# A routed two-layer MLP behind attention: logits of the last token tiles from x rows instead of a product of two weight matrices

## The chip, the cores and the metric

The kernel runs on one core of one Trainium2 chip. The metric is the device time of one execution in microseconds (us); lower is better.

## What is computed

Linear attention feeds a dense MLP (`w_in`, `w_out`), whose rows x feed a mixture of 8 experts. Each token goes to one expert: the token and expert with the largest logit are taken first, and an expert that has its 288 tokens is closed.

```python
def _moe_ref(x, w_in, w_out):
    h = x @ w_in
    g = h * np.clip(h + 3.0, 0.0, 6.0) / 6.0
    return g @ w_out
def _moe2_ref(x, w_gate, w1, w2):           # x: 2304 x 512, 8 experts, cap = 288
    logits = x @ w_gate
    order = np.argsort(-logits.flatten())
    for idx in order:                       # greedy: best pair first
        tok, e = idx // E, idx % E
        if assigned[tok] >= 0 or counts[e] >= cap: continue
        assigned[tok] = e; counts[e] += 1
    for e in range(E):
        mask = assigned == e
        out[mask] = np.maximum(x[mask] @ w1[e], 0.0) @ w2[e]
```

## The kernel before

All matrix products are split in three: each operand is a high and a low part, and `mm3` (lines 207 to 210) issues high by high, low by high, high by low. The program has four stages.

**Attention** (to about 200 us) leaves x transposed in `xT`, in 4 blocks of 512 tokens and a short one of 256. The 2304 tokens are 18 tiles of 128; tiles 16 and 17 are the short block.

**The dense MLP** runs over `steps`: five blocks by 16 slices f of the hidden width. A step (`step`, line 648) splits the next slice of `w_in` (`st_wi`: iH by ScalarE, iL by GpSimd) and of `w_out` (`st_wo`: oH, oL), does A (`st_A`: 12 matmuls into a buffer called kv or s, then r, the product, gH and gL by ScalarE and VectorE) and, two steps behind, B (`st_B`: 3 matmuls for each token tile into pj). After its last slice each tile's sum is copied out of PSUM to `xs` (`st_x`, line 568), of which there are XS = 3 buffers, and stored to `xd` in DRAM. PSUM has four pj buffers, one for each tile of a long block: the next block's B cannot begin on a buffer before its copy is done.

**Logits.** For tiles 0 to 13, `st_dot` (line 578) has VectorE multiply x with the eight columns of the gate (`wgb`) and sum, 8 instructions for each tile; they read `xs`, for tiles 12 and 13 the PSUM buffer itself. Tiles 14 to 17 (LT = 14) use x·w_gate = g·(w_out·w_gate). In block 1 `st_wgT` and `st_wgp` (lines 584 to 598) make w_out·w_gate: in each of 16 steps 4 transposes of `w_out` (L588), a copy by ScalarE (L590), 4 small matmuls (L596, 8 rows in the trace), and two small splits (L597, L598). In block 3 and the short block `st_lg` (line 600) then adds 2 matmuls in each step (L611, L612). So the logits of the short block are known once its g are: A keeps all of them (`kept`), and B of the short block is taken out of the steps and becomes `rest` (line 682), 96 matmuls (L696).

**Routing and experts.** `finds` (line 796) looks for the members of one expert after another. `begin` makes keys from the logits; `closest` (line 758) takes six rounds, five or six bits each: VectorE compares (cmp, L755), TensorE counts with 18 small matmuls (L771), VectorE tests (ge, L773), TensorE spreads the result (L776), VectorE takes it in (L780, L783). Then slots (L857, L858), one-hot rows (OH, L889), 18 small matmuls (L893) and the list of rows idx (L898). `finds` stops at names ("cmp5", "ge", "mem", "OH", "first"), and the tables GAP0 and GAP say after how many pieces of other TensorE work it is taken up again. For expert 0 the other work is `rest`: TensorE's order is as written there, so L696 stands between the rounds. At "mem" the first two parts of the expert's w1 are requested on SP; after "first" `fetch_x` gathers the expert's rows from `xd` by three indirect DMAs on GpSimd (L917) and then requests the other weights, behind a small VectorE instruction that needs the gathered rows (L923). `prep` transposes the rows (L943), and `mlp` runs the expert; the searches for the next experts stand between its matmuls (`visit`, line 1045). N1 = 6 pieces of the second search stand ahead of `prep`.

Of the kernel before, what the change touches and what calls it, by code (L numbers as in the profile page):

```python
# [6 lines left out]
F32 = mybir.dt.float32  # L7
F32R = mybir.dt.float32r
# [12 lines left out]
def fused(tc, q, k, v, omega, w_in, w_out, w_gate, w1, w2, out):  # L21
# [25 lines left out]
    HPF, RP, N1, GAP = 400, 30, 6, dict(cmp0=12, cmp5=4, cmp6=5, ge=1, mem=6, OH=7)  # L47
# [6 lines left out]
    with ctx:  # L54
# [23 lines left out]

        wgp = cp.tile([P, 16, 2, 8], F32R, name="wgp")
# [469 lines left out]
        keep, on_pool, on_dve = {}, [], []  # L549

        def kept(f):

            if f % 8 == 0:
                keep["H"] = xp.tile([P, 2048], F32, tag="x", name="gHk")
            if f % 4 == 0:
                keep["L"] = (xp.tile([P, 4, 2 * P], F32, tag="x4", name="gLk", bufs=1).rearrange("p c n -> p (c n)") if f == 0 else
                             mb.tile([P, 512, 2], I32, tag="stg", name="gLk", bufs=CV[0]).rearrange("p n w -> p (n w)"))
            n = 2 * P
            return (keep["H"].bitcast(F32R)[:, (f % 8) * n:(f % 8 + 1) * n], keep["L"].bitcast(F32R)[:, (f % 4) * n:(f % 4 + 1) * n])
# [8 lines left out]
        def st_x(t, acc):  # L568
# [15 lines left out]
        def st_wgT(f):  # L584
# [8 lines left out]
        def st_wgp(f, wT):
            pg = ps("tp")
            for c in range(4):
                nc.tensor.matmul(pg[:, :8], wT[:, c * P:(c + 1) * P], wgn[:, c], start=c == 0, stop=c == 3, skip_group_check=True)  # L596
            nc.scalar.copy(wgp[:, f, 0], pg[:, :8])  # L597
            nc.vector.tensor_tensor(wgp[:, f, 1], pg[:, :8], wgp[:, f, 0].bitcast(F32), ALU.subtract)  # L598

        def st_lg(i):  # L600

            ib, f = steps[i]
            gH, gL = gs[i]
            if "lg" not in keep:
                keep["lg"] = ps("tp")
            nl = (NT - LT) * P

            o = keep["lg"][:16, 0:nl - 2 * P] if ib < NB else keep["lg"][:16, nl - 2 * P:nl]
            w = wgp[:, f].rearrange("p a e -> p (a e)")
            c = slice((LT - 4 * ib) * P if ib < NB else 0, len(blocks[ib]) * P)  # L610
            nc.tensor.matmul(o, w, gH[:, c], start=f == 0, stop=False, skip_group_check=True)  # L611
            nc.tensor.matmul(o, w, gL[:, c], start=False, stop=f == NF - 1, skip_group_check=True)  # L612
            if ib == NB and f == NF - 1:
                t8 = mp.tile([16, nl], F32, name="lgT", bufs=1)
                nc.vector.tensor_copy(t8, keep["lg"][:16, :nl])
                pt = ps("tp")
                for j in range(NT - LT):
                    nc.tensor.transpose(pt[:, 16 * j:16 * j + 16], t8[:, j * P:(j + 1) * P], ident[:16, :16])
                p4 = pt[:, 0:16 * (NT - LT)].rearrange("p (t a e) -> p t a e", t=NT - LT, a=2)

                nc.vector.tensor_copy(lg[:, LT:NT], p4[:, :, 0])
                nc.vector.tensor_scalar(lg[:, 0:LT], lg[:, 0:LT], 0.0, None, ALU.add)
# [488 lines left out]
```

## Time and profile before

| | us |
|---|---|
| median of 3 runs (lowest, highest) | 967.49 (965.32, 973.01) |
| the profiled execution | 971.14 |
| its span, first to last instruction | 969.4 |
| TensorE busy in the span | 901.8 (93%) |
| VectorE, ScalarE, GpSimd busy | 641.6, 496.2, 466.8 |

Busy shares are means over stages: the attention, the five MLP blocks (about 200 to 651 us), the wait for the first expert's rows, and the eight experts (670 us to the end) have limits of their own. A matmul's row shows its length in the pipeline, longer than the distance to the next; costs on TensorE are read from start to start.

### The profile page before, as it was taken

The page shows a single profiled execution, that of the slowest core. Times are in us where ns is not written, and L with a number is a line of the kernel's source. Part 1 is how long each engine was busy: PE and PEld are TensorE (multiplying, and loading weights), DVE is VectorE, ACT ScalarE, POOL GpSimd, SP SyncE. Part 2 cuts the span into 40 slices and gives each one's busy share as a digit, 9 for nine tenths or more (in the row PEclk, how much of TensorE's full clock was granted, in tenths as well). Part 3 has the DMA queues.
Part 4 walks back from the last instruction along what each step waited for, and adds up shares of the span by engine and source line. Part 5 has one row for each costly group of instructions (what it writes and reads, how often), then busy time and mean ns, then how long its engine had stood idle before and what let it go on. Part 6 is the DMA issues. An engine that isn't in the chain of part 4 may idle for free. (4 is left out here: it accounts for less than half of the span.)

```text
span 969.4 us, 16981 instructions
## 1 busy us (share of the span) xinstructions
PE 901.8 (93%) x6135; PEld 787.7 (81%) x6135; DVE 641.6 (66%) x1666; ACT 496.2 (51%) x1091; POOL 466.8 (48%) x435
## 2 busy tenths in 40 slices
PE   7999799989999999999999999985998999999996
PEld 6998698967778888878887888864997888889996
DVE  4779889868876653496259427765866857858442
ACT  5777788955545444534452447522343433434552
POOL 6669756327653433545444546302433444436542
PEclk9999899999999999999999999995999999989999
DMA  8855432012400000010000001006615426326600
GB/s 198 225 158 164 132 109 67 23 66 73 148 19 33 11 1 1 1 44 1 1 33 12 0 1 44 1 11 199 208 45 181 141 86 216 127 104 231 216 25 25
DMA packets 74852, 81.93 MB, mean 85 GB/s; under 512 B 27016, under 2 KB 59784, under 8 KB 74640
## 3 DMA queue, kind: packets, MB, share of 16 engines
q1 hardware_dynamic: 71536, 71.15, 23.1%
q0 software_dynamic: 3072, 9.44, 3.1%
q8 instruction: 48, 0.79, 0.3%
q10 hardware_dynamic: 160, 0.26, 0.1%
q14 instruction: 36, 0.29, 0.1%
HBM read 71.39 MB, written 9.45 MB: 83 GB/s over the span
## 5 line engine op out<-in xcount | busy, mean ns | idle before, releaser
L502 POOL TENSOR_TENSOR iL<-W,iH 128x512 fp32r<-128x512 f32 x80 | 112.9, 1412 | 96.5 <-ACT iH L501 86.8
L962 POOL TENSOR_TENSOR iL<-We,iH 128x512 fp32r<-128x512 f32 x63 | 84.3, 1339 | 135.1 <-ACT iH L959 129.1
L208 PE MATMUL kv<-xH,iH 128*128 128x512 f32 (+2 forms) x376 | 132.4, 352 | 1.8 <-ACT xH L520 1.8
L210 PE MATMUL kv<-xH,iL 128*128 128x512 f32 (+2 forms) x376 | 129.4, 344 | 2.6 <-POOL iL L502 2.6
L209 PE MATMUL kv<-xL,iH 128*128 128x512 f32 (+2 forms) x376 | 129.2, 344 | 0.9 <-DVE xL L521 0.9
L510 POOL TENSOR_TENSOR oL<-W,oH 128x512 fp32r<-128x512 f32 x48 | 66.2, 1380 | 95.8 <-ACT oH L509 95.6
L208 PE MATMUL pj<-oH,gH 128*128 128x512 f32 x256 | 103.1, 403 | 3.5 <-DVE xs L570 3.5
L210 PE MATMUL pj<-oH,gL 128*128 128x512 f32 x256 | 101.6, 397 | 0.0
L209 PE MATMUL pj<-oL,gH 128*128 128x512 f32 x256 | 101.4, 396 | 0.0
L501 ACT CAST iH<-W 128x512 fp32r<-128x512 f32 x80 | 49.7, 621 | 82.7 <-PE kv L209 48.8
L581 DVE SCALAR_TENSOR_TENSOR junk<-xs,wgb 128x512 f32<-128x512 f32 x96 | 89.4, 962 | 2.3 <-PE tp L596 2.2
L273 ACT ACTIVATE kp<-pj,bias 128x128 f32<-128x128 f32 x288 | 79.4, 412 | 17.9 <-DVE bias L265 14.4
L208 PE MATMUL pj<-hH,oH 128*128 128x288 f32 x256 | 84.3, 329 | 0.0
L210 PEld LDWEIGHTS kv<-xH,iL 128*128 128x128 f32 x376 | 72.0, 191 | 11.3 <-POOL iL L502 4.3
L208 PEld LDWEIGHTS kv<-xH,iH 128*128 128x128 f32 x376 | 71.9, 191 | 11.2 <-issue 3.5
L209 PE MATMUL pj<-hL,oH 128*128 128x288 f32 x256 | 77.3, 302 | 3.2 <-DVE hL L984 3.2
L959 ACT CAST iH<-We 128x512 fp32r<-128x512 f32 x64 | 39.5, 619 | 79.0 <-PE kv L209 30.6
L209 PEld LDWEIGHTS kv<-xL,iH 128*128 128x128 f32 x376 | 72.1, 192 | 8.5 <-DVE xL L521 1.2
L544 DVE SCALAR_TENSOR_TENSOR kv<-r,kv 128x512 f32<-128x512 f32 (+1 forms) x54 | 34.7, 643 | 65.9 <-ACT r L543 65.7
L210 PE MATMUL pj<-hH,oL 128*128 128x288 f32 x256 | 76.7, 299 | 0.0
L182 POOL TENSOR_TENSOR stg<-cg,stg 128x512 f32<-128x512 f32 x32 | 41.8, 1305 | 71.6 <-issue 30.4
L509 ACT CAST oH<-W 128x512 fp32r<-128x512 f32 x80 | 49.5, 620 | 41.8 <-PE pj L210 25.7
(400 smaller groups left out, 2393.3 us busy)
## 6 DMA issues: line engine op xcount, KB each, us to landing
We<-in_moe_w_dram SPq DMA_DIRECT2D x64, 512.0 KB, 7.4
stg<-in_moe_w_in_dram SPq DMA_DIRECT2D x16, 512.0 KB, 4.9
stg<-in_moe_w_out_dram SPq DMA_DIRECT2D x16, 512.0 KB, 3.6
ld<-in_k_dram SPq DMA_DIRECT2D x8, 512.0 KB, 4.9
vf<-in_v_dram SPq DMA_DIRECT2D x32, 128.0 KB, 3.4
ld<-in_q_dram SPq DMA_DIRECT2D x8, 512.0 KB, 4.8
xd<-xs SPq DMA_DIRECT2D x16, 256.0 KB, 2.4
wgb<-wgd SPq DMA_DIRECT2D x1, 2048.0 KB
```

What stands on the lines that cost most here:

```text
L182: nc.gpsimd.tensor_tensor(lf, g.bitcast(F32), lf, ALU.mult)
L208: nc.tensor.matmul(o, aH, bH, start=first, stop=False, skip_group_check=True)
L209: nc.tensor.matmul(o, aH, bL, start=False, stop=False, skip_group_check=True)
L210: nc.tensor.matmul(o, aL, bH, start=False, stop=last, skip_group_check=True)
L273: nc.scalar.activation(kp[:, i, j], pjs[s // 4][:, s % 4], AF.Exp, bias=bias[:, i, j:j + 1])
L501: nc.scalar.copy(iH, wi)
L502: on_pool.append(nc.gpsimd.tensor_tensor(iL, wi, iH.bitcast(F32), ALU.subtract).ins)
L509: nc.scalar.copy(oH, wo)
L510: (nc.gpsimd if (ib > 0 if ib < NB else f >= OD) else nc.vector).tensor_tensor(oL, wo, oH.bitcast(F32), ALU.subtract)
L581: nc.vector.scalar_tensor_tensor(junk, x, 1.0, wgb[:, e], ALU.mult, ALU.mult, accum_out=d)
L959: nc.scalar.copy(iH, wi)
L962: (nc.vector if first and f == 0 else nc.gpsimd).tensor_tensor(iL, wi, iH.bitcast(F32), ALU.subtract)
```

## The change

The product w_out·w_gate and all that makes or uses it is gone. The short block runs like the others: A and B in the same step, g in the usual buffers. The logits of tiles 12, 13, 16 and 17 are now made from x rows by TensorE: `st_lT` transposes the row tile (4 transposes), copies it, and `st_lg` multiplies with the gate (4 matmuls). Tiles 12 and 13 are done in two steps of the short block; 16 and 17 after its end, with one copy on ScalarE and one on VectorE. Tiles 14 and 15 now go by VectorE from PSUM, as 12 and 13 did. The first search stands after all this, with nothing between its pieces. `xs` has four buffers. The x rows of tile 16 are stored on SP ahead of expert 0's first weights. N1 is 4, and GAP changes: 3 or 4 pieces after a compare, 2 after "ge", and at most 3 anywhere until two experts are found. In the short block oL alternates between GpSimd and VectorE.

```diff
-    OD, WG, ND, NE, XS = 16, 18, 3, 3, 3
-    LB, LL, GB = 2, 3, 3
-    LT = 14
-    GAP0 = dict(begin=32, cmp5=6, cmp6=7, ge=2, mem=9, OH=12)
+    ND, NE, XS = 3, 2, 4
+    LB, GB = 2, 3
+    LT = (12, 13, 16, 17)
-    HPF, RP, N1, GAP = 400, 30, 6, dict(cmp0=12, cmp5=4, cmp6=5, ge=1, mem=6, OH=7)
+    HPF, RP, N1, GAP = 400, 30, 4, dict(cmp0=12, cmp5=3, cmp6=4, ge=2, mem=6, OH=7)
...
-            (nc.gpsimd if (ib > 0 if ib < NB else f >= OD) else nc.vector).tensor_tensor(oL, wo, oH.bitcast(F32), ALU.subtract)
+            (nc.gpsimd if (ib > 0 if ib < NB else f % 2 == 0) else nc.vector).tensor_tensor(oL, wo, oH.bitcast(F32), ALU.subtract)
...
-            if t < 16:
-
-                if t < LT:
-                    dots.extend((acc if t >= 12 else x, lg[:, t, e:e + 1], e) for e in range(8))
+            if t in LT:
+                xrow.append((t, x))
+            else:
+
+                dots.extend((acc if t >= 14 else x, lg[:, t, e:e + 1], e) for e in range(8))
...
+        def st_lT(x, copy):
 
             pt = ps("big")
             for c in range(4):
-                nc.tensor.transpose(pt[:, c * P:(c + 1) * P], w_rows(f)[:, c * P:(c + 1) * P], ident)
...
+                nc.tensor.transpose(pt[:, c * P:(c + 1) * P], x[:, c * P:(c + 1) * P], ident)
+            xT = mp.tile([P, DM], F32, tag="junk", name="xTt", bufs=2)
+            copy(xT, pt)
+            return xT
+
+        def st_lg(t, xT):
+
             pg = ps("tp")
             for c in range(4):
...
+                nc.tensor.matmul(pg[:, :8], xT[:, c * P:(c + 1) * P], wgn[:, c], start=c == 0, stop=c == 3, skip_group_check=True)
+            nc.vector.tensor_scalar(lg[:, t], pg[:, :8], 0.0, None, ALU.add)
...
-                if ib == 1:
-                    wT = st_wgT(f)
+                if xrow:
+                    t, x = xrow.pop(0)
+                    xT = st_lT(x, nc.scalar.copy)
...
-            if LB <= i < NB * NF + LB:
-                if i - LB >= (NB - 1) * NF and LT < 4 * NB:
-                    st_lg(i - LB)
+            if LB <= i:
                 st_B(i - LB)
...
+            elif i + 1 - LB == len(steps):
+                st_dot(len(dots))
+                nc.vector.tensor_scalar(lg[:, 0:12], lg[:, 0:12], 0.0, None, ALU.add)
+                nc.vector.tensor_scalar(lg[:, 14:16], lg[:, 14:16], 0.0, None, ALU.add)
+                xTs = [st_lT(x, copy) for (t, x), copy in zip(xrow, (nc.scalar.copy, nc.vector.tensor_copy))]
+                for (t, x), xT in zip(xrow, xTs):
+                    st_lg(t, xT)
...
-            for _ in more:
...
+        with tc.manual_schedule(engines={ET.PE}), tc.high_priority(offset=400):
+            while True:
+                z = next(route)
+                if z == "mem":
+                    fetch_w(0, rs[0], 0, Z0)
+                if z == "first":
+                    break
...
-                wait[0] = GAP.get(z, 0)
+
+                wait[0] = min(GAP.get(z, 0), 3) if found[0] < 2 else GAP.get(z, 0)
```

Three places show what moves. TensorE, the end of the first round of the first search, before (tp holds the counts, pj the short block's sums):

```order
L771 LDWEIGHTS cmp_6575
L771 MATMUL tp_6584<-oh_6573,cmp_6575 32x8
L696 MATMUL pj_6500<-oL_6532,gHk_6034 128x512
L696 MATMUL pj_6500<-oH_6531,gLk_6184 128x512
L696 MATMUL pj_6499<-oH_6541,gHk_6034 128x512
L776 LDWEIGHTS onesu_4509
L776 MATMUL tp_6606<-ge_6604,onesu_4509 128x8
```

The same place now (L714 is L771 of before, L719 is L776):

```order
L714 LDWEIGHTS cmp_6458
L714 MATMUL tp_6467<-oh_6456,cmp_6458 32x8
L719 LDWEIGHTS onesu_4284
L719 MATMUL tp_6488<-ge_6486,onesu_4284 128x8
L714 LDWEIGHTS cmp_6494
L714 MATMUL tp_6496<-oh_6456,cmp_6494 32x8
```

The short block's B no longer stands between the pieces of the search.

VectorE at the start of block 2, before (L570 is the copy of a tile to xs, L581 a dot, L544 and L546 belong to A):

```order
L544 SCALAR_TENSOR_TENSOR kv<-r,kv 128x512
L570 COPY xs<-pj 128x512
L581 SCALAR_TENSOR_TENSOR junk,lg<-xs,wgb 128x512
L546 TENSOR_TENSOR gL<-kv,gH 128x512
L581 SCALAR_TENSOR_TENSOR junk,lg<-xs,wgb 128x512 x5
L544 SCALAR_TENSOR_TENSOR s_4621<-r,s_4621 128x512
L581 SCALAR_TENSOR_TENSOR junk,lg<-xs,wgb 128x512 x2
L546 TENSOR_TENSOR gL<-s_4621,gH 128x512
L570 COPY xs<-pj 128x512
```

The same place now (L548 is the copy, L562 a dot, L532 and L534 belong to A):

```order
L532 SCALAR_TENSOR_TENSOR kv<-r,kv 128x512
L548 COPY xs<-pj 128x512
L562 SCALAR_TENSOR_TENSOR junk,lg<-xs,wgb 128x512
L534 TENSOR_TENSOR gL<-kv,gH 128x512
L548 COPY xs<-pj 128x512
L562 SCALAR_TENSOR_TENSOR junk,lg<-xs,wgb 128x512 x4
```

The second copy stands behind one dot instead of eight.

VectorE in the second search, at the small instruction that needs the gathered rows (L923), before:

```order
L783 SCALAR_TENSOR_TENSOR v__7061<-v__7032,dk,dg 128x36
L755 TENSOR_TENSOR cmp<-v__7061,ta 128x576
L773 TENSOR_SCALAR ge<-tp 32x8
L923 SCALAR_TENSOR_TENSOR e_6950<-xg,ei 1x1
L780 TENSOR_REDUCE dk<-tp 128x1
```

The same place now (L866 is L923, L698 the compare, L716 the test):

```order
L723 TENSOR_REDUCE dk<-tp 128x1
L726 SCALAR_TENSOR_TENSOR v__6812<-v__6774,dk,dg 128x36
L866 SCALAR_TENSOR_TENSOR e_6730<-xg,ei 1x1
L698 TENSOR_TENSOR cmp<-v__6812,ta 128x576
L716 TENSOR_SCALAR ge<-tp 32x8
```

It moved from the third round to the second, ahead of that round's compare.

## Rows read from the trace of the kernel before

**Rows 1.** The page: granted TensorE clock in tenths, 40 slices of 24.2 us.
```profile
PEclk9999899999999999999999999995999999989999
```

**Rows 2.** Blocks 1, 2, 3: us, PE, PEld, DVE, ACT, POOL busy, clock, DMA, GB/s.
```profile
303.00:411.00 108.00, 108.00 (x561) 90.99 (x561) 59.04 (x138) 50.82 (x100) 45.17 (x55) 1.00 0.03 11
411.00:503.00 92.00, 90.23 (x385) 73.07 (x384) 54.46 (x102) 40.93 (x71) 44.65 (x33) 0.98 0.03 12
503.00:594.60 91.60, 89.85 (x417) 72.33 (x416) 54.70 (x103) 40.47 (x72) 44.46 (x33) 1.00 0.03 12
```

**Rows 3.** Timeline of TensorE in one step of block 1: start, length, instruction.
```profile
342.66 0.60 PE L588 MATMUL kv<-ident,W 128*128 128x128 f32 x4
343.01 0.48 PE L208 MATMUL pj<-oH,gH 128*128 128x512 f32 x1
...
345.88 0.95 PE L596 MATMUL tp<-wgn,wT 128*128 128x8 f32 x8
346.69 0.48 PE L208 MATMUL s<-xH,iH 128*128 128x512 f32 x1
```

**Rows 4.** Timeline of TensorE in block 2; in brackets idle before, and releaser.
```profile
421.94 0.50 PE L208 MATMUL pj<-oH,gH 128*128 128x512 f32 x1 [1.77 <-DVE xs L570]
...
451.97 0.39 PE L210 MATMUL s<-xH,iL 128*128 128x512 f32 x1
```

**Rows 5.** Timeline of VectorE in block 2.
```profile
421.21 0.68 DVE L570 COPY xs<-pj 128x512 f32<-128x512 f32 x1
...
448.62 0.69 DVE L546 TENSOR_TENSOR gL<-kv,gH 128x512 fp32r<-128x512 f32 x1 [0.66 <-ACT gH L545]
```

**Rows 6.** Groups of VectorE, 411 to 450 us: busy us, mean ns | idle before.
```profile
L581 DVE SCALAR_TENSOR_TENSOR junk<-xs,wgb 128x512 f32<-128x512 f32 x32 | 29.6, 973 | 0.0
```

**Rows 7.** Timeline of TensorE from the short block to the first expert.
```profile
596.53 0.28 PE L208 MATMUL kv<-xH,iH 128*128 128x256 f32 x1
...
599.41 0.28 PE L611 MATMUL tp<-gHk,wgp 128*16 128x256 f32 x1
...
599.64 0.28 PE L208 MATMUL kv<-xH,iH 128*128 128x256 f32 x1
...
630.34 0.59 PE L771 MATMUL tp<-oh,cmp 128*32 128x8 bf16 x18 [1.02 <-issue]
...
633.68 0.61 PE L771 MATMUL tp<-oh,cmp 128*32 128x8 bf16 x18
...
650.79 0.39 PE L696 MATMUL pj<-oH,gLk 128*128 128x512 f32 x1
...
659.54 0.64 PE L771 MATMUL tp<-oh,cmp 128*32 128x8 bf16 x18 [4.40 <-DVE cmp L755]
...
664.07 0.65 PE L771 MATMUL tp<-oh,cmp 128*32 128x8 bf16 x18 [1.04 <-DVE v__7061 L783]
...
668.16 0.90 PE L943 MATMUL kv<-ident,xg 96*128 96x96 f32 x4 [1.96 <-DMA xg<-xd,idx]
...
670.05 0.61 PE L208 MATMUL kv<-xH,iH 128*128 128x288 f32 x1
```

**Rows 8.** Timeline of VectorE in the first search.
```profile
626.78 0.30 DVE L728 TENSOR_REDUCE mx__6558<-lg 128x18 f32<-128x144 f32 x1
...
627.66 0.69 DVE L510 TENSOR_TENSOR oL<-W,oH 128x512 fp32r<-128x512 f32 x1 [0.57 <-ACT oH L509]
...
655.37 0.16 DVE L898 SCALAR_TENSOR_TENSOR idx<-tp,lo 96x3 int32<-96x3 f32 x1
```

**Rows 9.** Timeline of GpSimd at the first gather.
```profile
660.66 1.11 POOL L917 DMA_INDIRECT xg<-xd,idx  x1 [30.66 <-PE tp L776]
```

**Rows 10.** Timeline of TensorE at the second search's end.
```profile
687.55 0.19 PE L857 MATMUL tp<-mem,ta 128*128 128x36 bf16 x1
...
691.52 1.08 PE L893 MATMUL tp<-mv,OH 128*96 128x6 bf16 x18 [0.48 <-DVE OH L889]
```

**Rows 11.** Waits of TensorE, 672 to 930 us: us in total, times, longest.
```profile
PE tp L776 <- DVE ge L773: 4.8, 7, 1.9
```

More of the change, by code (lines that the diff above doesn't have):

```diff
@@ L547, in st_A @@
             gs[i] = gH, gL
[L549 to L559, printed above, removed]
+        on_pool, on_dve = [], []
         def x_rows(t):
@@ L594, in st_wgp @@
+        def st_lg(t, xT):
             pg = ps("tp")
             for c in range(4):
[L596 to L622, printed above, removed]
-                nc.vector.scalar_tensor_tensor(lg[:, LT:NT], p4[:, :, 1], 0.0, lg[:, LT:NT], ALU.add, ALU.add)
@@ L656, in step @@
                     st_w(i + 1)
-                if i + 2 - LB < NB * NF and i + 2 - LB > 0:
+                if i + 2 - LB > 0:
                     j = i + 2 - LB
@@ L671, in step @@
                         st_xb(ib + 1, c)
-            if LB <= i < NB * NF + LB:
-                if i - LB >= (NB - 1) * NF and LT < 4 * NB:
-                    st_lg(i - LB)
+            if LB <= i:
                 st_B(i - LB)
-            if i < len(steps) and ib == 1:
-                st_wgp(f, wT)
-            if i >= NB * NF + LL:
-                st_lg(i - LL)
-            st_dot((ND if i <= NB * NF else NE) if i < len(steps) else len(dots))
-        def rest():
-            base = NB * NF
-            for f in range(2):
-                wos[base + f] = st_wo(f)
-            a = [ps("acc") for _ in range(2)]
-            for f in range(NF):
-                if f + 2 < NF:
-                    wos[base + f + 2] = st_wo(f + 2)
-                gH, gL = gs[base + f]
-                oH, oL = wos.pop(base + f)
-                for j in range(2):
-                    c = slice(j * P, (j + 1) * P)
-                    for z, (x, y) in enumerate(((gH, oH), (gH, oL), (gL, oH))):
-                        nc.tensor.matmul(a[j], x[:, c], y, start=f == 0 and z == 0, stop=f == NF - 1 and z == 2, skip_group_check=True)
-                        if f == NF - 1 and z == 2:
-                            st_x(16 + j, a[j])
-                        yield
-        more = rest()
+            if i < len(steps):
+                if t is not None:
+                    st_lg(t, xT)
+                st_dot(ND if i <= NB * NF else NE)
+            elif i + 1 - LB == len(steps):
[4 more added lines that the diff above has]
+                for (t, x), xT in zip(xrow, xTs):
+                    st_lg(t, xT)
         i = 0
@@ L706, in fused @@
                 i += 1
-        while i < len(steps) + LL:
+        while i < len(steps) + LB:
             step(i)
@@ L1023, in fused @@
         route = finds()
-        wait, placed = [GAP0["begin"]], False
-        with tc.manual_schedule(engines={ET.PE}):
-            for _ in more:
-                wait[0] -= 1
-                if wait[0] < 0 and not placed:
-                    with tc.high_priority(offset=400):
-                        z = next(route)
-                    placed, wait[0] = z == "first", GAP0.get(z, 0)
-                    if z == "mem":
-                        fetch_w(0, rs[0], 0, Z0)
-            with tc.high_priority(offset=400):
-                while not placed:
-                    z = next(route)
-                    placed = z == "first"
-                    if z == "mem":
-                        fetch_w(0, rs[0], 0, Z0)
+        with tc.manual_schedule(engines={ET.PE}), tc.high_priority(offset=400):
[5 more added lines that the diff above has]
+                    break
         mb_.close()
```

27 lines of the change are left out of this document (9 added, 18 removed).

## Prediction

> **What bounds the kernel now.** I read the page first (clock and busy slices), then the stretches of the dense MLP, the timelines of TensorE and VectorE at the block starts, and last the timelines from the short block to the first expert. TensorE is the bound nearly everywhere: it is busy for all 108.00 us of block 1 and all but 1.8 us of block 2 and of block 3 [rows 2]. Two kinds of place are not TensorE's. At the start of blocks 2 and 3 it waits for a tile's copy to xs, 1.77 us in block 2 [rows 4]; the whole idle time of block 3, 91.60 - 89.85 = 1.75, is of the same size [rows 2]. And from the last matmul of the short block (650.79 + 0.39 = 651.2) to the first of expert 0 (670.05) there are 18.9 us [rows 7] in which TensorE has only small matmuls and the clock falls to 0.5, the 1.2 GHz level, in the slice from 678 back to 654 us [rows 1]. That wait ends last on a DMA: the gathered rows arrive at 668.16 [rows 7]. Their request came at 660.66 [rows 9], 5 us after the list idx was there (655.53) [rows 8]; the x rows of tiles 16 and 17 are written only after 651 us, so the gather waited for their stores.
>
> So every instruction that leaves TensorE in the MLP blocks is time won, and every microsecond added between the short block and expert 0 is paid in full.
>
> **The product w_out·w_gate goes.** In a step of block 1 the 4 transposes take 343.01 - 342.66 = 0.35 us and the 8 small matmuls 346.69 - 345.88 = 0.81; the matmul behind each lasts 0.48 instead of 0.39 [rows 3, 4], 0.09 more, twice. That is 1.34 us a step, 16 steps: **-21.4 us**. Check: about 14.5 of the 16 steps lie in the stretch of block 1, 19.4 us; block 1 is 108.0, and block 2 without its 1.77 of waiting and the 1.8 that clock 0.98 costs in 92 us is 88.4, a difference of 19.6 [rows 2]. The copies and splits beside it (ScalarE, VectorE) go too; no engine there waits for them, 0.
>
> **Four xs buffers.** In block 2 VectorE's second copy starts at 421.21 [rows 5], and TensorE starts right behind it [rows 4]: with three buffers this copy needs the first one back, so it stands behind 8 dots; now it stands behind one. What can be won is 1.77 + 1.8 of low clock in block 2 and 1.75 in block 3, 5.3 us. Not all of it: VectorE is full there, 32 dots of 973 ns [rows 6], and the last of them delay gL. The slowest gL ends at 448.62 + 0.69 = 449.3 [rows 5]; its slice's B follows the A that ends at 452.2 [rows 4], a slack of 2.9 us. With TensorE 3.6 earlier it is 0.7 late. Three blocks now look like this (block 1 has lost the work that gave VectorE time): 2.1 back. **-3.2 us**, with 0 lost (-5.3) and three stalls of 3.6 instead of two (+5.5) as its ends.
>
> **The products with g go in block 3.** The two matmuls of a step take 599.64 - 599.41 = 0.23 us [rows 7], 16 times: **-3.7 us**.
>
> **The short block.** From 596.53, where its third A starts, to 651.2 it takes 54.7 us [rows 7]. Now: 14 A's of 12 matmuls at (599.41 - 596.53) / 24 = 0.12 [rows 7], 20.2; 96 matmuls of B at (345.88 - 343.01 - 0.09) / 12 = 0.232 [rows 3], 22.2; two tiles of logits at 1.34, the same instructions as above, 2.7; 0.4 for hand-overs, an estimate. 45.5 us, **-9.2**. What goes are the products with g and six rounds of the search that stood between. The dots of tiles 14 and 15 take the place of those of 12 and 13, the same 16: 0. As each step now has B as well, ScalarE, VectorE and GpSimd have 2.8 us for what they did at 1.66.
>
> **From there to expert 0.** The cover is gone: nothing of TensorE stands between the pieces of the first search. Step by step:
> - The logits of 16 and 17: copy 0.68 [rows 5], transposes 0.60, copy 0.68, small matmuls 0.95 [rows 3], 0.2 for the add, five hand-overs of about 0.13: 3.8 us. An estimate from those rows; ends 2.8 (the copies overlap) and 6.
> - The search took 626.78 to 655.53, 28.75 us, under cover [rows 8]. A round took 633.68 - 630.34 = 3.34 there and (664.07 - 659.54) / 2 = 2.27 in the second search, where nothing stood between [rows 7]: six rounds are 6.4 shorter. The weight split at 627.66 with its wait, 1.2 [rows 8], goes too. 21.1 us; ends 19 and 28.75.
> - The gather: the x rows are now stored some 20 us ahead of idx, so it starts with idx, 0.2; then 668.16 - 660.66 = 7.5 [rows 7, 9].
> - L923, the instruction that waits for the gathered rows, now stands ahead of the second search's second compare (front, third place), and in TensorE's order that round's L771 and L776 stand ahead of the transposes of the rows. After the rows are there, compare, counts, test and spread come first: about three quarters of a round, 1.75. Ends: 0 (the rows come before that round) and 2.27. Behind L923 on VectorE nothing else waits that expert 0 needs.
> - Transposes and splits to the first matmul, 670.05 - 668.16 = 1.9 [rows 7].
>
> Sum 36.3 instead of 18.9: **+17.4 us**. SP asks for the weights behind the same two events as before, the tile 16 store ahead of them now being early: 0.
>
> The rows show a count of 18 small matmuls at 0.59 and 0.61 under full clock and 0.64 and 0.65 after idling [rows 7], a twentieth more. The Trainium skill, page "TensorE: Matmul & The Clock Gate", section "HAM oscillation — how this bites in real kernels", says that gaps throw the array back to half its clock. Taken for all matmuls of the uncovered search, some 5 us of them by the lengths in the rows, it would add 5; by the rows it adds 0.3, and I go by the rows. That expert 0 starts at the low level is so before and after.
>
> **The experts.** N1 and the gaps move the searches between the matmuls. After L857 of the second search came 24 matmuls and still 0.48 of waiting before L893, 691.52 - 687.55 = 4.0 us in all [rows 10]; now 12 matmuls stand there, so TensorE waits some 1.6 us longer, an estimate. Against it, each test gets three matmuls more of time before L776, where 4.8 us were waited in 7 cases [rows 11], and 0.4 off at most each would give back some 2. I take 0; ends -4.8 and +4.
>
> **Sum.** -21.4 - 3.2 - 3.7 - 9.2 + 17.4 + 0 = -20.1. The profiled execution took 971.14, which gives 951.0; the median of the runs lies 3.65 below it, so 967.49 - 20.1 = **947.4 us**, 2.1% less.
>
> **Rivals.**
> - *VectorE holds the block starts.* The dots read two operands from SBUF while GpSimd splits weights: a copy of this size takes 0.68 [rows 5], a dot 0.97 on average [rows 6]. With block 1's steps 1.34 shorter, VectorE falls behind in three blocks and TensorE waits in each, 3.6: +5.5 instead of -3.2, in all -11.4, 956.1. For it: VectorE is full, the slack is 2.9. Against: the copy that was waited for comes 6 us earlier. The Trainium skill, page "SBUF — State Buffer", section "Who interferes with whom", says that such an instruction and one of GpSimd that reads SBUF shut each other out; the longer dots agree with it.
> - *The uncovered search is no shorter than the covered one*, 28.75, since it is bound by hand-overs: +7.65, in all -12.4, 955.1. Against: 2.27 a round without cover. Together with the first, -3.7: 963.8, no difference that shows.
> - *Slower.* The stretch from the short block to expert 0 has no cover, so one slow link decides. All else wins 37.5 us, so the change loses once the stretch is over 56 us, 20 more than reckoned: rounds of 5.6 us, with an instruction in VectorE's order that waits for a transfer in each, as L923 does in the second search. At 7.5 us a round, +31: 978. Against: in the order of the first search no such instruction stands.
> - *More is won.* No lag at the block starts (-2.1), a search of 19 us (-2.1), gaps that pay (-4.8): 938.
>
> **Chances.** The forecast, -14 to -27, 0.62; one of the first two rivals 0.18; both, 0.13; slower by over 1%, 0.05; more won, 0.02. A measurement of this kernel tells about 1%, 9.7 us, from no change: faster by more 0.81, within 0.14, slower by more 0.05. The range goes from the last rival to the first two without their whole sum: 937 to 961.
>
> **What would show it.** No row of L588 or L596 and a block 1 of about 89 us; no wait of TensorE for xs; a short block that ends some 9 us sooner after its third A; then about 36 us to the first expert's matmul, rounds near 2.3 us, the gather's request within 1 us of idx. Wrong, if block 1 stays above 92 us, if a wait for gL or xs of some us shows at block starts, or if the stretch is nearer 50.

## The result

The changed kernel takes 955.84 us (median of 4 runs, 951.22 to 957.52), the kernel before, timed beside it, 969.07 (965.32 to 973.01): a ratio of 0.9855, 95% interval 0.9823 to 0.9888. It is 13.2 us faster where 20.1 were forecast. The profiled execution took 955.96 us with a span of 953.9, 15.5 less than the span before.

Lines of the kernel moved up by 4 to 57: the triple product is now L204 to L206, the copy to xs L548, the copy behind a transpose L571, the small matmuls of the logits L578; in the search the compare is L698, the counts L714, the test L716, the spread L719, mem L757 with L800, OH L832 with L836, idx L841; the gather is L860, the instruction that waits for it L866, the transposes of the rows L886.

The granted clock of the page, which still has one slice at 0.5, but now with 0.8 on either side of it and two more slices at 0.8 in the experts, where [rows 1] has one 0.8 behind its 0.5 (slices of 23.8 us):

```profile
PEclk9999899999999999999999999858998989999999
```

Then the stretches of the blocks, in the columns of [rows 2], and as a fourth row the experts from their first matmul to 17 us ahead of the end.

```profile
300.05:388.48 88.43, 88.43 (x385) 72.05 (x384) 56.52 (x123) 40.50 (x72) 46.39 (x55) 1.00 0.04 13
388.48:476.90 88.42, 88.42 (x385) 72.09 (x384) 53.67 (x102) 40.27 (x71) 43.41 (x33) 1.00 0.03 13
476.90:562.61 85.71, 85.71 (x385) 70.33 (x384) 52.71 (x103) 38.81 (x71) 41.37 (x32) 1.00 0.04 13
646.97:936.90 289.93, 270.71 (x2440) 253.88 (x2439) 183.01 (x634) 122.24 (x252) 126.83 (x104) 0.96 0.42 140
```

TensorE is busy for all of each block, at full clock: the waits at the block starts are gone, and with them the 0.98 of block 2. In the experts it stands idle for 289.93 - 270.71 = 19.2 us.

Next the timeline of TensorE from the short block to expert 0, which answers to [rows 7].

```profile
564.37 0.28 PE L204 MATMUL kv<-xH,iH 128*128 128x256 f32 x1
...
609.09 0.39 PE L206 MATMUL pj<-oH,gL 128*128 128x512 f32 x1
...
610.79 1.06 PE L578 MATMUL tp<-wgn,xTt 128*128 128x8 f32 x8
612.11 1.63 PE L578 MATMUL tp<-wgn,xTt 128*128 128x8 f32 x8 [0.26 <-DVE lg L579]
616.58 0.62 PE L714 MATMUL tp<-oh,cmp 128*32 128x8 bf16 x18 [2.85 <-issue]
...
618.65 0.64 PE L714 MATMUL tp<-oh,cmp 128*32 128x8 bf16 x18 [1.04 <-DVE cmp L698]
...
625.22 1.12 PE L714 MATMUL tp<-oh,cmp 128*64 128x8 bf16 x18 [1.34 <-DVE cmp L698]
...
633.97 1.60 PE L836 MATMUL tp<-mv,OH 128*96 128x6 bf16 x18 [2.28 <-DVE OH L832]
...
646.97 0.61 PE L204 MATMUL kv<-xH,iH 128*128 128x288 f32 x1
```

The third A of the short block starts at 564.37, its last matmul ends at 609.48: 45.1 us. From there to expert 0 it is 37.5. The same stretch on VectorE, as in [rows 8], and on GpSimd, as in [rows 9]:

```profile
614.17 0.30 DVE L671 TENSOR_REDUCE mx__6441<-lg 128x18 f32<-128x144 f32 x1
...
616.69 0.25 DVE L692 TENSOR_TENSOR dg<-di,ta 128x90 f32<-128x90 int32 x1
...
635.80 0.16 DVE L841 SCALAR_TENSOR_TENSOR idx<-tp,lo 96x3 int32<-96x3 f32 x1
...
639.43 2.01 DVE L692 TENSOR_TENSOR dg<-di,ta 128x90 f32<-128x90 int32 x1
...
642.91 0.15 DVE L866 SCALAR_TENSOR_TENSOR e<-xg,ei 1x1 int32<-1x1 int32 x1 [0.69 <-DMA xg<-xd,idx]
```

```profile
636.25 1.19 POOL L860 DMA_INDIRECT xg<-xd,idx  x1 [18.75 <-DVE lg L779]
...
640.04 1.28 POOL L905 TENSOR_TENSOR iL<-We,iH 128x512 fp32r<-128x512 f32 x1
```

The pieces are: logits 4.7 us (609.48 to 614.17; 4.1 when the same kernel ran again, e11), search 21.8 (to 635.96), request 0.3 behind idx instead of 5, the rows 6.7 behind the request, and 4.1 more to the first expert's matmul.

Last the waits of TensorE in the experts, in the columns of [rows 11].

```profile
PE kv L886 <- DMA xg<-xd,idx: 4.8, 5, 1.2
PE tp L836 <- DVE OH L832: 4.2, 3, 2.1
PE tp L714 <- DVE cmp L698: 3.4, 6, 1.1
PE tp L800 <- DVE mem L757: 3.0, 3, 1.7
PE tp L719 <- DVE ge L716: 1.3, 3, 0.7
```

The wait for ge went from 4.8 to 1.3, as the wider gap behind the test was priced, but three others stand in its place: in the kernel before, OH was waited for 0.5 us, mem 0.6, and its list has no row for cmp. The wait for the rows is a little longer than it was, and one for hL (the low part of an expert's hidden values), 0.5 now, was 3.2; the kernel before:

```profile
PE kv L943 <- DMA xg<-xd,idx: 3.9, 4, 1.4
PE pj L209 <- DVE hL L984: 3.2, 4, 1.3
```

Stage by stage, in us, with the kernels of the experiments. A block runs from its first copy to xs on ScalarE (the start column ends at the first of these), "to third A" from the last such mark to the third A of the short block, the short block from there to its last matmul, the stretch to the first matmul of expert 0, the experts to the end of the span.

| kernel | start | block 1 | block 2 | to third A | short | stretch | experts | span |
|---|---|---|---|---|---|---|---|---|
| before | 303.1 | 107.94 | 92.07 | 93.46 | 54.65 | 18.87 | 299.4 | 969.4 |
| changed | 300.1 | 88.43 | 88.42 | 87.47 | 45.11 | 37.49 | 306.9 | 953.9 |
| e1 | 300.8 | 88.42 | 88.43 | 87.46 | 45.11 | 40.23 | 294.0 | 944.5 |
| e2 | 301.7 | 88.42 | 88.43 | 87.47 | 45.11 | 39.48 | 297.2 | 947.8 |
| e3 | 302.0 | 107.86 | 88.43 | 87.46 | 45.16 | 36.51 | 307.0 | 974.4 |
| e4 | 300.2 | 92.04 | 90.50 | 89.53 | 45.40 | 37.37 | 311.3 | 966.3 |
| e5 | 301.1 | 88.43 | 88.43 | 87.46 | 45.12 | 36.22 | 309.1 | 955.8 |
| e6 | 300.7 | 88.43 | 88.42 | 87.47 | 45.10 | 38.39 | 299.1 | 947.6 |
| e7 | 301.2 | 88.42 | 88.43 | 87.47 | 45.10 | 36.61 | 311.1 | 958.3 |
| e8 | 301.3 | 88.43 | 88.42 | 87.46 | 45.11 | 37.01 | 301.3 | 949.0 |
| e9 | 301.4 | 88.42 | 88.43 | 87.46 | 45.11 | 37.95 | 293.6 | 942.3 |
| e10 | 301.3 | 88.43 | 88.43 | 87.46 | 45.12 | 40.36 | 308.5 | 959.6 |
| e11 | 299.9 | 88.43 | 88.43 | 87.46 | 45.10 | 37.05 | 307.2 | 953.6 |
| e12 | 301.2 | 88.43 | 88.42 | 87.47 | 45.10 | 45.18 | 293.3 | 949.1 |

The changed kernel, e3, e4, e7 and e11 have the same order of work in the experts, and their profiles give 306.9, 307.0, 311.3, 311.1 and 307.2 there: a part that scatters by 4 us, while an undisturbed block repeats to 0.02. The scatter is not one of waits. The experts of e11 and of e4, from their first matmul to TensorE's last:

```profile
646.41:945.20 298.79, 279.33 (x2504) 262.05 (x2502) 187.80 (x639) 124.65 (x258) 126.45 (x104) 0.96 0.41 136
655.02:957.90 302.88, 283.60 (x2504) 266.26 (x2502) 186.08 (x639) 124.35 (x258) 125.61 (x104) 0.95 0.41 134
```

TensorE is idle for 19.5 and 19.3 us; the same 2504 matmuls are busy 4.3 us longer in e4, where the granted clock is lower. In the stretch, too, kernels with one order differ, from 36.5 (e3) to 37.5.

### The profile page after: what moved, and what is told of

Its sections match the earlier page's. It is cut to its first block, busy times and chain, and to the rows that moved or that the text cites. A ratio compares the mean times of both kernels' runs of the same rounds, so it can differ in the third digit from the quotient of the medians.

```text
span 953.9 us, 16517 instructions
## 1 busy us (share of the span) xinstructions
PE 877.3 (92%) x5923; PEld 770.3 (81%) x5923; DVE 630.1 (66%) x1645; ACT 483.9 (51%) x1062; POOL 476.3 (50%) x443
## 5 line engine op out<-in xcount | busy, mean ns | idle before, releaser
L905 POOL TENSOR_TENSOR iL<-We,iH 128x512 fp32r<-128x512 f32 x63 | 87.9, 1395 | 141.9 <-ACT iH L902 129.3
L204 PE MATMUL kv<-xH,iH 128*128 128x512 f32 (+2 forms) x372 | 130.3, 350 | 1.8 <-ACT xH L511 1.8
L206 PE MATMUL kv<-xH,iL 128*128 128x512 f32 (+2 forms) x372 | 127.7, 343 | 2.6 <-POOL iL L496 2.6
L504 POOL TENSOR_TENSOR oL<-W,oH 128x512 fp32r<-128x512 f32 x56 | 72.9, 1302 | 104.3 <-ACT oH L503 104.3
L206 PE MATMUL pj<-oH,gL 128*128 128x512 f32 x288 | 113.8, 395 | 0.0
L204 PE MATMUL pj<-oH,gH 128*128 128x512 f32 x288 | 113.7, 395 | 0.0
L205 PE MATMUL pj<-oL,gH 128*128 128x512 f32 x288 | 113.4, 394 | 0.0
L269 ACT ACTIVATE kp<-pj,bias 128x128 f32<-128x128 f32 x288 | 79.1, 409 | 17.6 <-DVE bias L261 14.5
L562 DVE SCALAR_TENSOR_TENSOR junk<-xs,wgb 128x512 f32<-128x512 f32 x96 | 86.5, 948 | 0.0
L204 PE MATMUL pj<-hH,oH 128*128 128x288 f32 x256 | 84.1, 328 | 0.0
L206 PEld LDWEIGHTS kv<-xH,iL 128*128 128x128 f32 x372 | 71.6, 193 | 11.1 <-POOL iL L496 4.3
L204 PEld LDWEIGHTS kv<-xH,iH 128*128 128x128 f32 x372 | 71.4, 192 | 11.2 <-issue 3.0
L206 PE MATMUL pj<-hH,oL 128*128 128x288 f32 x256 | 76.9, 301 | 0.0
L532 DVE SCALAR_TENSOR_TENSOR kv<-r,kv 128x512 f32<-128x512 f32 (+1 forms) x53 | 34.0, 642 | 59.7 <-ACT r L531 59.6
L206 PE MATMUL s<-xH,iL 128*128 128x288 f32 (+2 forms) x204 | 68.6, 336 | 2.3 <-POOL iL L496 2.3
```

What stands on the lines that cost most here:

```text
L204: nc.tensor.matmul(o, aH, bH, start=first, stop=False, skip_group_check=True)
L205: nc.tensor.matmul(o, aH, bL, start=False, stop=False, skip_group_check=True)
L206: nc.tensor.matmul(o, aL, bH, start=False, stop=last, skip_group_check=True)
L269: nc.scalar.activation(kp[:, i, j], pjs[s // 4][:, s % 4], AF.Exp, bias=bias[:, i, j:j + 1])
L504: (nc.gpsimd if (ib > 0 if ib < NB else f % 2 == 0) else nc.vector).tensor_tensor(oL, wo, oH.bitcast(F32), ALU.subtract)
L532: nc.vector.scalar_tensor_tensor(ph[:, :n], r[:, :n], 1.0, ph[:, :n], ALU.min, ALU.mult)
```

## The experiments

Each ratio is to the kernel before in the same comparison, with its 95% interval.

**e1 and e2: is it the spacing of the searches that made the experts longer?** e1 puts all of it back, e2 only the six steps ahead of expert 0.

```diff
 e1
-HPF, RP, N1, GAP = 400, 30, 4, dict(cmp0=12, cmp5=3, cmp6=4, ge=2, mem=6, OH=7)
+HPF, RP, N1, GAP = 400, 30, 6, dict(cmp0=12, cmp5=4, cmp6=5, ge=1, mem=6, OH=7)
-wait[0] = min(GAP.get(z, 0), 3) if found[0] < 2 else GAP.get(z, 0)
+wait[0] = GAP.get(z, 0)
 e2
-HPF, RP, N1, GAP = 400, 30, 4, dict(cmp0=12, cmp5=3, cmp6=4, ge=2, mem=6, OH=7)
+HPF, RP, N1, GAP = 400, 30, 6, dict(cmp0=12, cmp5=3, cmp6=4, ge=2, mem=6, OH=7)
```

> The changed kernel with the search spacing of the kernel before: six steps of the second search ahead of expert 0 instead of four, the old gaps (cmp5 4, cmp6 5, ge 1), and no cap of 3 on a gap. Nothing else differs. Theory (the spacing costs the experts their time): from expert 0's first matmul to the end of the span 300 us (298 to 302) instead of 306.9, the stretch ahead of it 1.9 us longer for one more round, the span near 949. Rival (the experts are longer since they start at a low clock behind an uncovered stretch, and stalls cost more): 305 to 309 us for the experts, the span near 956.

> The changed kernel with six steps of the second search ahead of expert 0 instead of four; new gaps and the cap stay. Theory (cap and gaps are the larger part of the cost): the waits for mem and OH in expert 0, 2.9 us in all, stay, one round of some 0.9 us leaves it; experts 304 to 306 us, the stretch +1.9, span 953 to 955. Rival (the number of steps ahead is the whole of it): experts 299 to 301 us, span near 949.

Measured: e1 949.62 us, 0.9783 (0.9730 to 0.9836); e2 949.80 us, 0.9776 (0.9728 to 0.9824). The experts took 294.0 and 297.2, the stretch 2.7 and 2.0 more. In e1 the spacing theory holds, by more than expected; but its profile is of the fastest of its four runs, and e6, with the same spacing, has 299.1. In e2 it is the rival that holds, by more than it said: two steps more ahead bring nearly all of it, though cap and gaps stay. The waits of TensorE in e2's experts show how:

```profile
PE tp L836 <- DVE OH L832: 4.1, 3, 2.0
PE tp L714 <- DVE cmp L698: 4.0, 6, 0.9
```

These two are as long as in the changed kernel, and cost little; the wait for gathered rows, 4.8 us there, has no row left in e2. (In e1 it is 1.9 in 3.) With one round fewer ahead, a search ends later beside its expert, and the request of the next expert's rows comes later. The third expert's rows are requested 73.4 us behind the first expert's first matmul in the changed kernel (720.41), 3.1 ahead of their first transpose (723.55); in e2 70.8 behind it (721.42, with 650.63 for that matmul), 6.6 ahead (728.01). What such a wait does can be seen in the changed kernel's second expert, in the timeline of TensorE:

```profile
723.55 0.30 PE L886 MATMUL kv<-ident,xg 96*128 96x96 f32 x1 [1.18 <-DMA xg<-xd,idx]
724.88 0.30 PE L886 MATMUL kv<-ident,xg 96*128 96x96 f32 x1 [1.04 <-DMA xg<-xd,idx]
726.06 0.42 PE L886 MATMUL kv<-ident,xg 96*128 96x96 f32 x1 [0.87 <-DMA xg<-xd,idx]
...
729.09 0.44 PE L206 MATMUL pj<-hH,oL 128*128 128x288 f32 x1
729.33 0.44 PE L204 MATMUL pj<-hH,oH 128*128 128x288 f32 x1
...
733.34 0.29 PE L204 MATMUL kv<-xH,iH 128*128 128x288 f32 x1
733.47 0.29 PE L205 MATMUL kv<-xL,iH 128*128 128x288 f32 x1
```

and in its stretches (columns as in [rows 2]; the clock stands before the last two):

```profile
723.50:729.00 5.50, 3.54 (x15) 2.93 (x16) 1.26 (x4) 0.60 (x2) 1.59 (x2) 0.64 0.18 63
729.00:733.00 4.00, 4.00 (x37) 3.78 (x36) 2.08 (x7) 1.61 (x4) 0.00 (x0) 0.64 0.00 0
```

Three waits close together, 3.1 us in all, and the granted clock is 0.64 on average in both stretches: matmuls of 288 columns follow each other every 0.24 us (729.09 to 729.33), at 1.2 GHz, until about 732, and then every 0.13.

**e8: the transposes later.** With them at the very end of an expert, the rows have more time.

```diff
-FZ, FS, PZ, PS = 6, 2, 56, 2
+FZ, FS, PZ, PS = 6, 2, 60, 1
```

> The changed kernel with the transposes of the next expert's rows at steps 60 to 63 of an expert instead of 56 to 62; search spacing as changed. Theory A (TensorE's waits for the gathered rows, 4.8 us in 5 cases, and the low clock after them are the larger part of what the experts got longer by): those waits go, experts 299 to 302 us instead of 306.9. Theory B (they are a small part, or come back as a wait of the next expert's first products for the splits of the rows): experts 304 to 310.

Measured: 950.07 us, 0.9789 (0.9754 to 0.9824), experts 301.3: theory A in its number. The waits for the rows and the stretch in the second expert where the changed kernel had 0.64:

```profile
PE kv L886 <- DMA xg<-xd,idx: 1.6, 2, 0.9
```

```profile
725.00:731.00 6.00, 4.43 (x48) 3.85 (x47) 5.00 (x11) 2.88 (x8) 1.35 (x2) 1.00 0.16 52
```

3.2 us less of waiting, 5.6 us less of time: each microsecond of waiting for the rows cost 1.75 in this pair of profiles, the rest being matmuls at the low level. The size is uncertain, as the experts scatter by 4 us with the clock alone; the medians fall by 5.8. And the kernel before had 3.9 us of these waits too, so e8 also takes out a cost that was there already; it does not show that they alone are the 7.5.

**e3 and e4: the two larger terms of the blocks, each put back.** e3 adds the product of w_out and w_gate to block 1 (its result unused), e4 takes the fourth buffer.

```diff
 e3
+wT = st_wgT(f) if ib == 1 else None
...
+if ib == 1:
+    st_wgp(f, wT)
 e4
-ND, NE, XS = 3, 2, 4
+ND, NE, XS = 3, 2, 3
```

> The changed kernel with the product w_out by w_gate put back into block 1 (4 transposes, 8 small matmuls, a copy and a split a step, 16 steps); its result is not used. The step as priced (1.34 us, 16 times): block 1, from one block's first xs copy to the next, 88.4 to about 109.8, the span +21.4 (20.5 to 22.3). Rival (its copies and splits also held ScalarE or VectorE, so its removal won more than TensorE's part): +23 to +26.

> The changed kernel with three buffers of x rows instead of four. Theory (all that the blocks won beyond the products came from the fourth buffer): +7.0 us, 1.1 in the first two blocks, 3.65 in block 2, 2.3 up to the short block, and waits of TensorE for xs of near 1.8 us come back at the block starts. Term on record: +3.2 to +5.3. Rival (with the product gone the copy that was waited for comes early enough even with three): +0 to +2.

e3: 977.39 us, 1.0053 (1.0029 to 1.0078). Block 1 is 19.4 longer, 14.5 steps of 1.34, and 1.9 lie ahead of it (302.0 for 300.1); the span is 20.5 longer. The step as priced is right, and with four buffers the product costs no wait.

e4: 967.06 us, 0.9965 (0.9942 to 0.9988). The waits between 300 and 617 us, and block 1:

```profile
PE pj L204 <- DVE xs L548: 5.3, 3, 1.8
```

```profile
300.18:392.22 92.04, 90.26 (x385) 73.16 (x384) 57.36 (x123) 41.19 (x72) 47.16 (x55) 0.98 0.03 12
```

Three starts wait now where two did before: without the product, block 1 does too. One of the three also costs 1.8 of low clock. In the blocks that is 3.6 + 2.1 + 2.1 + 0.3 = 8.0, so the first theory is near in its sum (7.0), but not in how it lay over the blocks. The other 4.4 us of e4's span lie in the experts, whose order and idle time did not change: the clock. Beside the kernel before, which has three buffers too, e4's part to the third A is 93.46 - 89.53 = 3.9 shorter: the products with g, priced at 3.7.

**e5 to e7: the stretch ahead of expert 0.** In e5 and e6 L866, and the weight requests that wait for it, come behind the second (third) round of the second search; e6 stands on e1's spacing.

```diff
 e5, e6
-fetch_x(0, rs[0])    (the gather, L866, and the weight requests)
+fetch_x(0, rs[0])    (the gather alone)
...
 for _ in range(N1):
     next(route)
+with tc.issue_after(lastv[0].ins):
+    fetch_w2(0, rs[0])
 e7
-for (t, x), xT in zip(xrow, xTs):
-    st_lg(t, xT)
+pg = ps("tp")
+for j, xT in enumerate(xTs):
+    for c in range(4):
+        nc.tensor.matmul(pg[:, 8 * j:8 * j + 8], xT[:, c * P:(c + 1) * P], wgn[:, c], ...)
+nc.vector.tensor_scalar(lg[:, 16:18], pg[:, :16].rearrange("p (t e) -> p t e", t=2), 0.0, None, ALU.add)
```

> The changed kernel with L866, the VectorE instruction that waits for the gathered rows, and the weight requests behind it put after the second search's second round instead of ahead of its second compare. Theory (the order on record, 1.75 us): the round runs while the gather is under way, the transposes of the rows start within 0.3 us of the arrival of the last of them, the stretch from the last matmul of the short block to expert 0 goes from 37.5 to 35.7. The experts' part keeps its order, 303 to 310. Rival (the round ends no sooner, since VectorE is held by something else there): stretch 37.2 to 37.8.

> The kernel of e1 (search spacing of before, six steps ahead) with the same move of L866, behind the third round. Beside e1's stretch of 40.2: its first count starts 3.7 us after idx and three rounds take near 6.5, the rows arrive 7.4 after their request, so 1.3 us can be won: stretch 38.9, experts 294 to 299, 1 us less than e1. Rival (the weights, asked for later, then arrive late for expert 0): the first expert's part over 36.5 us where e1 had 35.4.

> The changed kernel with the logits of tiles 16 and 17 in one PSUM tile and one add, so that the second tile's small matmuls don't wait for the first tile's add. Theory (the one buffer costs that wait, and the second add): 4.7 us from the last matmul of the short block to the start of the search become 3.8 to 4.1; the stretch 36.6 to 36.9. Rival (the low clock on the 128-column products sets the length): 4.5 or more.

e5: 957.04 us, 0.9871 (0.9841 to 0.9902), stretch 36.2. The stretch is 1.3 shorter, but 0.6 of that lies in the logits (4.1, as in e11), where nothing was changed; from the request to the first transpose it is 7.85 instead of 8.54 (8.68 in e11), so the order cost 0.7 to 0.8, not 1.75. The transposes did not follow the arrival of the rows: L866's counterpart found them there without waiting, so the two rounds end last. The first of them holds a dg of 2.01 us like the one at 639.43 above.

e6: 948.11 us, 0.9777 (0.9746 to 0.9808), stretch 1.8 less than e1's, 0.5 of it in the logits and 1.3 behind the request, as forecast; expert 0 as fast.

e7: 957.17 us, 0.9868 (0.9836 to 0.9900); from the last matmul to the search 3.7 instead of 4.7. Only 0.4 of that is the one buffer, as e11, with the order of the changed kernel, takes 4.1. Its second tile's small matmuls, which took 1.63 above:

```profile
611.99 1.06 PE L578 MATMUL tp<-wgn,xTt 128*128 128x8 f32 x8 [0.26 <-DVE lg L579]
```

The other 0.6 is the clock: it falls to the low level at 612.4 in the first profile, ahead of most of these matmuls, and at 615.3 in e11, behind them. So the theory's number is met, but for the larger part by the clock that the rival named. Neither e5 nor e7 shows in the total, where e11 has 0.9870.

**e9: what helped, together**, with e1's spacing, e6's order, e7's bank and e8's late transposes.

> The changed kernel with what helped so far in one: the search spacing of the kernel before with six steps ahead (e1), L866 behind the third round (e6), one bank for the last logits (e7), the transposes at steps 60 to 63 (e8). If the parts add: stretch 37.5 (e6's 38.4 less 0.9), the experts 293 to 297 (the waits for gathered rows gone, at 1.5 us for each us waited), span near 943, a median near 945. If e1's spacing has already taken what e8 took: experts 298 to 301, span 946 to 949.

945.40 us, 0.9749 (0.9709 to 0.9789), experts 293.6: the first forecast in its numbers, and this kernel beats both others. What the late transposes add here is not shown: e1 had 294.0 without them and e6 299.1, and from e6 to e9 the median falls by 2.7, where e8 alone had brought 5.8. **e11, the changed kernel again** beside it:

> The changed kernel as it is, beside e9 and e10: what a second profile of one order of instructions gives. If the experts' part differs from run to run by more than the blocks do, its 306.9 us are one draw of 303 to 311 (e4, e5 and e7, with the same order there, had 311.3, 309.1 and 311.1); the blocks 88.4 each to 0.02.

956.88 us, 0.9870 (0.9831 to 0.9910). Its experts took 307.2, 0.3 off the first profile, so a draw does not have to differ; with e4 and e7 the scatter is 306.9 to 311.3. That e1, e9 and e12 lie 13 below and e6 8 below is no scatter.

**e10 and e12: does the low clock lengthen the uncovered search?** Extra transposes of the identity fill TensorE's waits there; nobody reads them.

```diff
 z = next(route)
+if z in BUSY:
+    keep_busy(BUSY[z])
...
+BUSY = dict(cmp0=24, cmp5=8, cmp6=11, ge=1, mem=15, OH=19)    (e10)
+BUSY = dict(cmp0=13, cmp5=7, cmp6=9, ge=0, mem=12, OH=16)     (e12)
```

> The changed kernel with extra transposes of the identity, read by nobody, on TensorE wherever the first search and the first rounds of the second leave it waiting for VectorE (8 to 24 a place). Theory (the low clock in the uncovered search is what made the counts of 64 and 96 columns 1.12 and 1.60 us instead of 0.73 and 1.08 and the second L578 1.63): these rows go back to 0.73 and 1.08, the clock stays at 1.0, the stretch goes from 37.5 to 34 to 36, and expert 0 starts at full clock. Rival (the lengths belong to those shapes when nothing runs beside them, or the fillers stand in the way): the rows stay, stretch 37.5 or more.

> The kernel of e9 with fewer extra transposes of the identity than e10 had (7 to 20 a place, none ahead of the spreads L722), so that they end before VectorE has the next operand. If e10 lost its gain since the fillers stood in the way: counts of 64 and 96 columns at 0.73 and 1.08 (0.8 and 0.5 us won), no count starts later than in e9, the stretch from 37.95 to 36 to 37, expert 0 from its first matmul to its first hH 4.4 instead of 4.9, a span 1 to 2 us under e9's 942.3, a median of 943 to 945. Rival (what the clock gives is lost at the places where fillers and the search share PSUM banks and the queue): stretch 38 or more, no gain.

e10: 959.57 us, 0.9880 (0.9838 to 0.9922). TensorE's timeline in the first search:

```profile
614.28 4.48 PE L742 MATMUL kv<-ident 128*128 128x128 f32 x24
618.69 0.61 PE L714 MATMUL tp<-oh,cmp 128*32 128x8 bf16 x18
...
619.63 1.09 PE L742 MATMUL s<-ident 128*128 128x128 f32 x8
...
627.22 0.73 PE L714 MATMUL tp<-oh,cmp 128*64 128x8 bf16 x18
```

e12: 951.48 us, 0.9807 (0.9768 to 0.9847). The same places:

```profile
613.72 2.66 PE L749 MATMUL kv<-ident 128*128 128x128 f32 x13
616.72 0.62 PE L717 MATMUL tp<-oh,cmp 128*32 128x8 bf16 x18 [0.35 <-PE kv L749]
...
617.68 1.76 PE L749 MATMUL kv<-ident 128*128 128x128 f32 x7
...
627.79 1.12 PE L717 MATMUL tp<-oh,cmp 128*64 128x8 bf16 x18
```

In e10 the clock came back in the first search: the 64-column counts take 0.73 again instead of 1.12, and a filler 0.14 (1.09 / 8). But the first 24 stand ahead of the first count, which starts 4.3 us behind the logits' last matmuls instead of 2.8; with the faster counts behind it the search is 0.7 longer (22.5). In the second search's rounds the clock fell again (0.25 for a filler), and with fillers ahead of the rows' transposes these start 11.3 us behind the request instead of 8.5 or 8.7: the stretch is 40.4. So the theory is right on the rows of the first search and the rival on the time. In e12, with fewer, the clock stayed down: a filler takes 0.25 (1.76 / 7), seven of them more than the 1.04 us that TensorE had to wait, the counts stay at 1.12, the search takes 27.4 instead of 21.8, and the stretch is 45.2, 7 more than e9's. The rival's number (38 or more) holds, but not its reason, as there was nothing from the clock to lose; fillers are no gain in either form.

## Why the prediction was right, and where it was off

Direction and range hold: 955.8 in 937 to 961. The number is partly luck: -13.2 lies just outside the -14 to -27 that had 0.62, nearer to what either of the first two rivals gave (-11.4, -12.4) than to the -20.1, though neither's mechanism came. By the spans it is -15.5, in which errors cancel: blocks, short block and start gave 4.1 us more than forecast, stretch and experts cost 8.7 more. Its own terms against what the traces show:

| term | forecast | measured |
|---|---|---|
| product w_out·w_gate | -21.4 | -21.5 (107.94 - 88.43 in block 1, 2.0 for 1.5 steps ahead of it); put back in e3, +19.4 in block 1 |
| four xs buffers | -3.2 | -5.9 |
| products with g in block 3 | -3.7 | taken as priced; not run alone, but e4 beside the kernel before gives -3.9 |
| short block | -9.2 | -9.5 |
| stretch to expert 0 | +17.4 | +18.6 |
| experts | 0 | +7.5 |
| start of the span, not forecast | 0 | -1.0 (303.1 to 300.1, less the 2.0); it scatters from 299.9 to 301.7 without e3 |
| sum | -20.1 | -15.5 by the spans |

**Buffers.** Block 2 gave 3.65, and the part to the third A 6.0, of which 3.7 are the products with g: 5.9, a little over the end of 5.3. The step that failed is "0.7 late", so "2.1 back". The gL in question, and the matmul that needs it:

```profile
425.31 0.69 DVE L534 TENSOR_TENSOR gL<-s,gH 128x512 fp32r<-128x512 f32 x1 [0.65 <-ACT gH L533]
```

```profile
426.49 0.40 PE L206 MATMUL pj<-oH,gL 128*128 128x512 f32 x1
```

It ends at 426.0, 0.5 ahead of that matmul: the slack nearly went, but not below nothing, so the first rival (VectorE holds the block starts) did not come. The forecast took the slack up to the first matmul of B, 2.9; but gL is needed only by the third of the triple, in the kernel before at

```profile
452.66 0.40 PE L210 MATMUL pj<-oH,gL 128*128 128x512 f32 x1
```

3.35 behind the 449.31 at which that gL ended. And the 32 dots in such a stretch, [rows 6], take 948 ns instead of 973, 0.8 us in all: 3.35 + 0.8 - 3.65 = 0.5. e4 shows that the buffer is worth more to the change than to the kernel before, 8.0, as block 1 would wait too.

**Stretch.** The forecast steps are there one by one: logits 3.8 came out at 4.7 (0.4 the one bank, e7, and 0.6 the clock, e11), the search 21.1 at 21.8, the request 0.2 at 0.3, the gather 7.5 at 6.7, order and transposes 3.65 at 4.1. A round of 32 columns took 618.65 - 616.58 = 2.07, so the second rival (28.75) fell. The small matmuls were priced by the 32-column counts, a twentieth; those of 64 and 96 columns took 1.12 and 1.60 instead of the 0.73 of e10 and the 1.08 of [rows 10], about half again, 2 × 0.39 + 0.52 = 1.3 us. The granted clock did fall to half, 0.5 in the slice of the page, as the Trainium skill says of gaps ("TensorE: Matmul & The Clock Gate", section "HAM oscillation — how this bites in real kernels"); but with the 0.6 of the logits 1.9 us is as much as the rows show of it, where the forecast priced 0.3: the +5 reckoned by it did not come, since the small counts hardly changed.

**The experts: the step that failed.** "I take 0; ends -4.8 and +4." The step priced two things, the waits behind L857 and those for ge. The second came as priced, even better: -3.5. For the first, in the timeline of TensorE as in [rows 10]:

```profile
667.62 0.18 PE L800 MATMUL tp<-mem,ta 128*128 128x36 bf16 x1 [1.74 <-DVE mem L757]
...
670.75 1.08 PE L836 MATMUL tp<-mv,OH 128*96 128x6 bf16 x18 [1.23 <-DVE OH L832]
```

The wait ahead of L836 is 0.75 longer, not 1.6, but one of 1.74 for mem, which was not in the step, stands ahead of L800. The step priced one search, and three have these waits: OH and mem together cost 7.2 us of idle time where the kernel before had 1.1. They come with the cap and the gaps: with both, in e2, OH has 4.1 and mem 1.2, without, in e1, 0.5 and 0.6. The waits for cmp, 3.4 us behind the narrower gap, were not in the step either. But N1 and the gaps also set when a search ends, and so when the next expert's rows are requested, when TensorE waits for them, and how often the clock then falls. None of that was in the sum. The experts of the kernel before, as a stretch:

```profile
670.05:952.40 282.35, 267.67 (x2421) 251.76 (x2420) 185.76 (x630) 122.72 (x252) 125.56 (x104) 0.97 0.43 146
```

TensorE's idle time there was 282.35 - 267.67 = 14.7 and is now 19.2; its busy time is 3.0 longer, at 0.96 of the clock instead of 0.97, with one more search round among the experts. So 4.5 of the 7.5 are waits: OH, mem and cmp 9.5 more and the rows 0.9 more, ge 3.5 and hL 2.7 less. Of the 3.0, some 2.2 are the clock, an estimate: it stands at its low level for 23.5 us of the experts instead of 19.1, and there matmuls of 288 columns go at 0.24 instead of 0.13; the rest is about the round. e1 and e2 show that the spacing is the cause: with six steps ahead the 306.9 become 294.0 and 297.2, against 2.0 to 2.7 in the stretch, and the medians fall by 6. Which of the waits make the clock fall stays open, and this part scatters by 4.

## What to carry to other kernels

When a change moves a search, a prefetch or any chain that feeds the next stage, follow it to its last consumer: price the request that it issues and how long ahead of its use that now lies, not only the waits at the pieces that were moved. A wait on the main engine costs more than its length where the clock falls behind it, here some 1.75 us for each in e8, so a few close together are worth more than the table of waits shows. Read the stages apart: blocks that repeat to 0.02 us settle an edit in one run, where the total hid it in the scatter of the experts. Run the unchanged order twice before a step of half a microsecond is put down to an edit: e11 showed that most of what e7 seemed to win was the clock.

## What the runs showed of the hardware that was not expected

- **The low level costs by shape.** Eighteen counts took 0.64 instead of 0.61 us with 32 columns of weights, but 1.12 instead of 0.73 with 64 and 1.60 instead of 1.08 with 96.
- **Little idle time, much time.** Waits of 1.18, 1.04 and 0.87 us close together left the clock at 0.64 on average from 723.5 to 733 us; e8 with 0.9 at most in the same place kept 1.00, and e2 with as long waits for OH and cmp, none for rows, had 0.98 over the experts.
- **A small VectorE instruction of 2 us.** dg, a product over the digits of the keys, takes 0.25 us at 616.69 and 2.01 at 639.43, where GpSimd issues a gather and then splits a weight (640.04 to 641.32); it ends at 641.44, 0.1 behind the split. It reads two operands from SBUF. The Trainium skill, page "SBUF — State Buffer", section "Who interferes with whom", says that such an instruction and one of GpSimd that reads SBUF lock each other out for a whole instruction; the ends in these rows agree, but no run took the split away. In e3 the split ends ahead of dg (662.09), dg takes 0.25, and the instructions just ahead of it are held instead, until 662.21. The dots agree too: in the changed kernel 30 of the 96 that read two operands from SBUF take over 0.8 us, all 30 beside a split of GpSimd, and end 0.55 behind it; of the 16 that read one of them from PSUM 12 stand beside a split, and none takes over 0.69. The 1.8 us of dg are covered in the changed kernel, since L866 behind that round still waits 0.69 for the rows; in e5, where the rounds end last, they stand in the chain to expert 0.
